# Moving the key tail's scores forward in an attention + MoE kernel: from behind the fourth score unit to behind the second

## The chip, the cores and the metric

One core of a Trainium2 chip; the jobs ran on different chips, each with the kernel before in the same rounds. The metric is the device time of one execution in microseconds (us). Where ratios are given, they are the mean time of one kernel's fast runs over that of the other's of the same rounds, so they are not quite the ratios of the medians quoted beside them; the interval is a 95% one.

Engines are named as in the profile: PE is TensorE's matmuls, PEld its weight loads, ACT is ScalarE, DVE is VectorE, POOL is GpSimd, SP is SyncE.

## The reference

Attention with a relative position bias, then a layer of two matmuls with a "snake" activation. Batch 8, heads 8, sequence 576, head size 64; hidden sizes 512 and 2048.

```python
scores = (q @ k.transpose(0, 1, 3, 2)) / np.sqrt(64) + bias[head, |i - j|]
attn   = softmax(scores)
x      = (attn @ v)            # rearranged to 4608 x 512
h      = x @ w_in              # 4608 x 2048
g      = h + np.sin(alpha * h) ** 2 / (alpha + 1e-9)
out    = g @ w_out             # 4608 x 512
```

## The kernel before

Heads are handled in pairs: four head pairs a batch. The scores of a pair are computed transposed (keys on partitions), in six units. Units 0 to 3 are 128 keys each for 512 queries, unit 4 is the remaining 64 queries of those four key blocks, and unit "t" is the key tail: the last 64 keys of both heads, put together to 128 rows. Units 0 to 4 use 64 contraction rows and run as two half-array matmuls side by side (one per head). The tail uses a block-diagonal operand and all 128 rows. Every unit fills one score slot in PSUM (two banks). ScalarE takes the exponential out of the slot into a buffer `u`, and VectorE multiplies the part near the diagonal by the bias factor. Then come the attention-value matmuls (27 for the first 384 queries of a pair, 18 for the rest).

From the third batch on there are three score slots, dealt out in order of issue, and units are issued in groups of two that wait for both of their slots:

```python
        if t < LAG - 1:                       # first two batches: single units, two slots
            groups = [[(p, i)] for p in range(NP) for i in (0, 1, 2, 3, "t", 4)]
            nreg = 2
        else:                                 # (pair of the two, unit)
            groups = [
                [(y + p, i) for y, i in g] for p in range(0, NP, 2) for g in (
                    ((0, 0), (0, 1)), ((0, 2), (0, 3)), ((0, "t"),), ((0, 4), (1, 0)),
                    ((1, 1), (1, 2)), ((1, "t"),), ((1, 3), (1, 4)),
                )
            ]
            nreg = 3
        seq = [y for g in groups for y in g]
        ...
        r = seq.index(y) % nreg               # the unit's slot
        ...
        m.mode = "f" if g[0][1] == "t" else "r"   # full array, or two halves
```

Nothing is issued in the order of the text. Each piece is a task with a priority and an assumed duration; while the kernel is built, a greedy list scheduler deals the tasks onto the engines, and that order is then fixed. The output projection (`g @ w_out`, 16 matmuls of 128x512 for each of 36 row blocks) is *fill*: it is allowed wherever PE would otherwise wait, up to a quota while a batch's scores are issued:

```python
                    if t.fill:
                        if self.in_qk and self.used >= self.quota[0] + self.quota[1] * self.share:
                            continue
...
QUOTA = {2: (4, 26)}
QUOTA_ELSE = (8, 48)
...
            def mm(e, f=f):                   # output projection, one of 16
                if f == 0:
                    m.v = bank(mb.tag)
                full(m.v, gcell[b].v[:, f, 128 * a : 128 * a + 128], w_out16[:, f, :],
                     f == 0, f == NF - 1)
```

Attention stages (exponentials on ScalarE) and sine stages (sine and square) alternate, since ScalarE must load another function table in between (13 loads of 1.28 us in the trace).

The softmax here doesn't subtract the row's maximum and nothing guards it: scores larger than these inputs give would overflow.

## Time and profile before

| | |
|---|---|
| median of 6 runs | 392.96 us (392.29 to 393.67) |
| span of the profiled run | 392.2 us |
| PE / ACT / DVE busy | 378.4 / 323.9 / 262.0 us |
| granted TensorE clock, mean | 0.995 |

First the page of the profiled execution: span, busy time and share of each engine, two rows of the picture in 40 slices (tenths busy, tenths of granted clock), and the engine shares of the chain of waits that ended last.

```profile
span 392.2 us, 8566 instructions
PE 378.4 (96%) x3401; PEld 190.1 (48%) x3401; DVE 262.0 (67%) x587; ACT 323.9 (83%) x458; POOL 81.9 (21%) x96
...
PE   6989999999999999999999999999999999999995
...
PEclk9989999999999999999999999999999999999999
...
PE 86%; DMA 4%; DVE 4%; ACT 3%; POOL 1%; issue 1%; ACTq 0%; DVEq 0%
```

PE is busy almost everywhere after the first slice, and the chain is mostly PE work behind PE work. The next view gives busy time by stretch. The stretches are four attention stages, from one table load to the next; the columns are length, then busy time and instructions of each engine, granted clock, DMA share and GB/s.

```profile
157.40:180.10 22.70, 22.52 (x259) 11.32 (x258) 14.79 (x39) 21.15 (x26) 0.00 (x0) 1.00 1.39 149
197.30:220.10 22.80, 22.38 (x259) 11.20 (x258) 15.59 (x40) 21.05 (x26) 0.00 (x0) 1.00 0.96 111
237.10:259.60 22.50, 22.43 (x259) 11.56 (x258) 14.69 (x39) 20.89 (x27) 0.00 (x0) 1.00 0.44 106
277.20:299.60 22.40, 22.25 (x258) 10.97 (x256) 14.70 (x40) 21.04 (x25) 0.00 (x0) 1.00 0.25 50
```

Two engines are nearly full in these stages, PE at 99% and ACT at 93%.

PE's waits from 96.7 us on (who waited for whom: us in total, times, longest):

```profile
PE am L450 <- DVE xp L785: 0.8, 2, 0.4
PE sc L450 <- ACT u L705: 0.4, 1, 0.4
PE sc L450 <- DVE g L879: 0.3, 1, 0.3
PE am L450 <- DVE outs L538: 0.2, 1, 0.2
```

That is 1.7 us of idle time in 295. But a matmul's end is modelled: the Trainium skill, "Perfetto Trace Analysis", section "Tensor Engine Instruction (MATMUL, LD_WEIGHTS)", says that the profiler estimates it. In this trace a 128x512 matmul has 380 ns while the next one starts 216 ns after it, so the shown durations overlap and short stalls vanish under them. Starts are better. I therefore took the distances between the starts of successive matmul records, by kind of the two. From the third batch on, before:

| step | median ns | count |
|---|---|---|
| fill to fill (128x512) | 216 | 423 |
| fill to score (full array to two halves) | 311 | 31 |
| score to fill (two halves to full array) | 308 | 28 |
| the two half-array matmuls of one unit (512 columns) | 4 | 96 of 132 |
| attention-value to attention-value (65 columns) | 29 | 840 |

The 216 ns agree with the 215.7 ns that the Trainium skill, "TensorE: Matmul & The Clock Gate", section "Wait — 56ns, not 53.3ns?", gives for 512 columns on a warm array, and the 4 ns with the start distance in the diagram of its section "The mechanism" of Part 3 and with the issue overhead of about 4 ns a tile in the section after it, "Measured speedup vs the span model". The 308 and 311 ns show about 0.09 us for each change between half and full array. The Trainium skill, "TensorEngine Tiling (Array Packing)", section "Key Properties", says that changing the tiling mode drains TensorE; it gives no time.

The timeline of PE at the start of one attention stage (start us, time us, operation, count; Q is a score unit if its output is sc, fill if its input is g):

```profile
158.40 0.61 PE L450 MATMUL sc<-qT,kT 64*128 64x512 f16 x4
158.94 1.47 PE L450 MATMUL am<-w_out,g 128*128 128x512 f16 x6
160.34 0.61 PE L450 MATMUL sc<-qT,kT 64*128 64x512 f16 x4
160.88 0.39 PE L450 MATMUL am<-w_out,g 128*128 128x512 f16 x1
161.10 0.41 PE L450 MATMUL sc<-qT,kt 128*128 128x288 f16 x2
161.35 1.89 PE L450 MATMUL am<-w_out,g 128*128 128x512 f16 x8
```

Units 0 and 1, fill, units 2 and 3, fill, the tail (kt), fill. Fill stands wherever the next group still waits for a slot. And ScalarE in that stage, with its idle time and what ended it in brackets:

```profile
158.83 4.42 ACT L705 ACTIVATE u<-sc 128x1024 f16<-128x1024 f32 x5
163.50 4.02 ACT L705 ACTIVATE u<-sc 128x512 f16<-128x512 f32 x5 [0.25 <-PE sc L450]
167.74 1.51 ACT L705 ACTIVATE u<-sc 128x1024 f16<-128x1024 f32 x2 [0.21 <-PE sc L450]
```

After every few exponentials it waits 0.20 to 0.33 us in this stage for the next group's scores.

### The profile page before, as it was taken

The numbers are of one execution on the slowest core, as the hardware profiler recorded it, in microseconds if no ns is written. First come the engines' busy times: TensorE is split into PE (matmuls) and PEld (weight loads), VectorE is DVE, ScalarE is ACT, GpSimd is POOL, SyncE is SP. The second block draws the span as 40 slices with busy tenths as digits, with TensorE's granted clock in tenths as the row PEclk, the third lists the DMA queues.
The fourth block names the chain that finished last, engine by engine and source line by source line (L and its number), as shares of the span: only waits on it lengthen the run. The fifth ranks groups of instructions, "written<-read, shape, count | busy, mean of one in ns | idle before, by whom it ended". The sixth has DMA issues, their size and how long they took to land.

```text
span 392.2 us, 8566 instructions
## 1 busy us (share of the span) xinstructions
PE 378.4 (96%) x3401; PEld 190.1 (48%) x3401; DVE 262.0 (67%) x587; ACT 323.9 (83%) x458; POOL 81.9 (21%) x96
## 2 busy tenths in 40 slices
PE   6989999999999999999999999999999999999995
PEld 2456445644455554445445544554445444444442
DVE  3576987768576689567967895768676869429100
ACT  2976999979899999999989999999999969539211
POOL 5762963090004545001700310000000000000000
PEclk9989999999999999999999999999999999999999
DMA  9999999999726999991996497211014000020122
GB/s 170 211 204 219 207 171 158 166 171 148 92 59 83 158 155 157 158 166 47 150 170 101 34 93 166 68 33 42 27 43 59 17 28 29 27 80 2 57 76 80
DMA packets 148647, 41.99 MB, mean 107 GB/s; under 512 B 137784, under 2 KB 142992, under 8 KB 148608
## 3 DMA queue, kind: packets, MB, share of 16 engines
q0 software_dynamic: 89872, 19.04, 56.9%
q1 hardware_dynamic: 58512, 22.36, 30.3%
q8 instruction: 26, 0.43, 0.5%
q14 instruction: 13, 0.11, 0.1%
q10 hardware_dynamic: 224, 0.05, 0.1%
HBM read 37.76 MB, written 16.52 MB: 138 GB/s over the span
## 4 chain that ended last, share of the span: by engine, by line
PE 86%; DMA 4%; DVE 4%; ACT 3%; POOL 1%; issue 1%; ACTq 0%; DVEq 0%
PE sc L450 41%; PE am L450 34%; PE cb L450 5%; PE ca L450 5%; ACT u L705 2%; DMA m2r<-e_dram 2%; DMA e_dram<-e_sb 1%; DMA phi_sb<-phi_const 1%; DVE g L879 1%; DVE u L730 1%; ACT s L865 1%; DVE xn L785 1%; DVE outs L538 0%; DVE kT L538 0%; POOL mhr L471 0%
## 5 line engine op out<-in xcount | busy, mean ns | idle before, releaser
L705 ACT ACTIVATE u<-sc 128x1024 f16<-128x1024 f32 (+1 forms) x192 | 157.8, 898 | 14.4 <-PE sc L450 12.9
L450 PE MATMUL sc<-xT,w_in 128*128 128x512 f16 x576 | 132.3, 379 | 0.6 <-DVE g L879 0.5
L879 DVE SCALAR_TENSOR_TENSOR g<-sq,inv_a,sc 128x512 f16<-128x512 f16 x144 | 103.3, 746 | 22.1 <-PE am L450 14.7
L450 PE MATMUL am<-w_out,g 128*128 128x512 f16 x416 | 108.6, 380 | 0.3 <-DVE outs L538 0.2
L865 ACT ACTIVATE s<-sc,alphaT 128x512 f16<-128x512 f32 x144 | 92.7, 678 | 6.4 <-PE sc L450 5.0
L730 DVE TENSOR_TENSOR u<-u,m2r 128x512 f16<-128x512 f16 (+2 forms) x160 | 67.7, 438 | 32.4 <-ACT u L705 27.8
L450 PEld LDWEIGHTS <-w_in 128*128 128x128 f16 x576 | 55.3, 98 | 65.0 <-issue 1.3
L450 PEld LDWEIGHTS <-g 128*128 128x128 f16 x576 | 53.3, 98 | 64.1 <-issue 11.6
L450 PEld LDWEIGHTS <-u 128*128 128x128 f16 x1440 | 55.8, 98 | 19.2 <-issue 11.0
L450 PE MATMUL sc<-qT,kT 64*128 64x64 f16 (+1 forms) x512 | 50.8, 297 | 1.7 <-ACT u L705 0.9
L450 PE MATMUL am<-v,u 128*128 128x65 f16 x1152 | 51.2, 194 | 0.0
L872 ACT ACTIVATE sq<-s 128x512 f16<-128x512 f16 x79 | 49.2, 628 | 2.2 <-DVE g L879 0.5
L396 POOL DMA_DIRECT2D v<-in_v_dram x24 | 22.2, 1065 | 119.6 <-PE am L450 104.3
L874 DVE TENSOR_TENSOR sq<-s 128x512 f16<-128x512 f16 x65 | 27.4, 423 | 9.2 <-ACT s L865 8.8
L450 PE MATMUL am<-vh,u 128*128 128x130 f16 x144 | 32.2, 224 | 0.8 <-DVE xp L785 0.8
L450 PEld LDWEIGHTS <-kT 64*128 64x128 f16 x512 | 14.7, 96 | 28.5 <-issue 24.3
L785 DVE TENSOR_TENSOR xp<-am,rd 128x384 f16<-128x384 f32 (+1 forms) x48 | 23.6, 491 | 1.8
L784 DVE RECIPROCAL rd<-am 128x6 f32<-128x6 f32 (+1 forms) x56 | 10.5, 187 | 19.7 <-PE am L450 19.2
L450 PE MATMUL cb<-w_out,g 128*128 128x512 f16 x96 | 23.0, 380 | 0.0
L937 ACT ACT_TABLE_LOAD x13 | 16.7, 1283 | 0.2
L377 POOL DMA_DIRECT2D staged_q<-in_q_dram x6 | 15.5, 2583 | 3.6 <-DMA staged_q<-in_q_dram 3.6
L538 DVE COPY outs<-am 128x512 f32<-128x512 f32 x19 | 13.1, 688 | 4.3 <-PE am L450 4.1
(88 smaller groups left out, 175.6 us busy)
## 6 DMA issues: line engine op xcount, KB each, us to landing
out_dram<-outs SPq DMA_DIRECT2D x36, 256.0 KB, 2.2
staged_k<-in_k_dram POOLq DMA_DIRECT2D x6, 576.0 KB, 13.8
staged_q<-in_q_dram POOLq DMA_DIRECT2D x6, 576.0 KB, 19.7
v<-in_v_dram POOLq DMA_DIRECT2D x24, 128.0 KB, 7.0
w_in<-in_moe_w_in_dram POOLq DMA_DIRECT2D x4, 512.0 KB, 8.8
w_out<-in_moe_w_out_dram POOLq DMA_DIRECT2D x4, 512.0 KB, 10.7
w_out<-in_v_dram SPq DMA_DIRECT2D x4, 256.0 KB, 8.2
v1st<-in_v_dram POOLq DMA_DIRECT2D x4, 256.0 KB, 16.6
```

Source lines behind the costliest of these rows:

```text
L377: nc.gpsimd.dma_start(out=dst.ap()[t].rearrange("s (h d) -> s h d", h=H), in_=src[t].rearrange("h s d -> s h d"),)
L396: nc.gpsimd.dma_start(out=vs[t % 2][:, c, :, 0:D], in_=vp[128 * c : 128 * c + 128],)
L450: nc.tensor.matmul(out=out, lhsT=lhsT, rhs=rhs, start=start, stop=stop)
L538: k_of(e).tensor_copy(out=o, in_=i)
L705: nc.scalar.activation(out=o, in_=x, func=AF.Exp, scale=0.125)
L730: nc.vector.tensor_tensor(out=io, in0=io, in1=m2[:, 2 * p : 2 * p + 2, x0 : x0 + hi - lo], op=ALU.mult,)
L785: nc.vector.tensor_tensor(out=y.rearrange("p c (z d) -> p c z d", z=2), in0=a[:, :, :, 0:D], in1=r.unsqueeze(3).to_broadcast([128, nq, 2, ...
L865: nc.scalar.activation(out=s16.v, in_=h.v, func=AF.Sin, scale=alphaT[:, f : f + 1])
L872: nc.scalar.activation(out=sq.v, in_=s16.v, func=AF.Square)
L874: k_of(e).tensor_tensor(out=sq.v, in0=s16.v, in1=s16.v, op=ALU.mult)
L879: nc.vector.scalar_tensor_tensor(out=gcell[b].v[:, f, :], in0=sq.v, scalar=inv_a[:, f : f + 1], in1=h.v, op0=ALU.mult, op1=ALU.add,)
L937: nc.scalar.preload_act_table_set(name)
```

## The change

The intent: issue the tail, which is short on ScalarE, between the long units, so that another exponential covers the wait for the next group. Only the order of the groups changes.

```diff
@@ -630,8 +630,7 @@
                 [(y + p, i) for y, i in g] for p in range(0, NP, 2) for g in (
-                    ((0, 0), (0, 1)), ((0, 2), (0, 3)), ((0, "t"),), ((0, 4), (1, 0)),
-                    ((1, 1), (1, 2)), ((1, "t"),), ((1, 3), (1, 4)),
+                    ((0, 0), (0, 1)), ((0, "t"),), ((0, 2), (0, 3)), ((0, 4), (1, 0)), ((1, "t"),), ((1, 1), (1, 2)), ((1, 3), (1, 4)),
                 )
```

In the first head pair of two the tail moves from behind the fourth unit to behind the second; in the second head pair from behind the third to behind the first. The list lost one line, so the changed kernel's line numbers are one lower (L705 is L704 there).

What the scheduler makes of it, for PE in the first half of that attention stage (Q: half-array score matmuls, T: tail, A: attention-value, F: fill, with counts):

```
before  Q4 F6 Q4 F1 T2 F8 Q10 A27 Q4 F1 T2 F1 A18 F2 Q10
after   Q4 T2 F9 Q4 F6 Q10 F1 T2 F6 Q4 A27 F2 Q10
```

## The prediction

> **What bounds the kernel now.** TensorE. The page's first part has PE busy 378.4 us of a 392.2 us span, ACT 323.9, DVE 262.0. Windows by stage show PE busy, from 96.75 us on (where the changed order begins to act), 43.0 of 43.95 us in the third and fourth batches, then 22.3 to 22.5 of 22.4 to 22.8 us in each attention stage and nearly all of every sine stage. The granted clock is 1.00. The chain of waits puts 86% of the span on PE.
>
> "Busy" can hide stalls, so I took start-to-start distances of matmul records after 96.75 us. A 128x512 matmul follows another after 216 ns; the Trainium skill, "TensorE: Matmul & The Clock Gate", section "Wait — 56ns, not 53.3ns?", gives 215.7 ns warm, so PE streams at its rate. Going from half-array score matmuls (64 rows, in pairs) to full-array ones takes 308 instead of 216 ns, going back 311: 0.19 us a round trip. True stalls (steps over 60 ns longer than usual) sum to only about 3.7 us; the largest are 0.8 us twice.
>
> **What the change does.** It adds and removes no instruction. From the third batch on the order in each pair of head pairs becomes 0,1,tail,2,3,4 | 0,tail,1,2,3,4. The static scheduler then re-deals the fill matmuls (output projection) and attention-value groups around it; everything up to about 100 us is the same. Score buffers rotate over three slots in order of issue, so which unit uses which slot changes too.
>
> **Costed.**
> - Mode switches: both built orders have 190 changes between half- and full-array matmuls. Difference 0.
> - Scalar waits: ACT now waits three times per two head pairs, 0.20 to 0.33 us (timeline): a group of two units needs the slot whose exponential ended last, and only a short exponential (tail 0.57 us, 64-column unit 0.50) covers it. The new order has three such places too, perhaps 0.1 us longer each; off the critical path while PE has fill work.
> - Attention-value matmuls of even pairs: before, the tail came last and they followed directly; now unit 3 comes last, with its vector multiply (0.42 us) and a hand-over between: 0.5 us later, 12 times. Fill covers it; without fill up to 6 us.
> - Tails right behind a score group may hold PE about 0.13 us for their slot (one step of 441 ns instead of 308 is in the trace): 0 to 1.5 us, probably near 0.
> - Gain: at best the 3.7 us of stalls.
>
> The last 45 us keep their work and order nearly unchanged.
>
> **Predicted: 393.2 us, 391.0 to 395.8 in 8 of 10.** Faster by over 2%: 0.01; within: 0.97; slower by over 2%: 0.02.
>
> **What would show each step.** Right: PE busy stays at 378 +- 1.5 us and its idle time at 12 to 16, the steps of 308 and 311 ns stay equal in number, stages change by under 0.5 us each with mixed signs, the first 99 us agree to 0.3 us. Wrong: long PE steps before attention-value matmuls (waiting for DVE) or tails (waiting for ACT), or attention stages all longer by over 0.5 us.
>
> **What would make it wrong.** The scheduler works with its own durations; where it thinks a slot free too early, in-order PE stalls, and 24 tails times 0.3 us would be 7 us. Or fill is used up earlier, leaving holes in the sine stages. Or the new order removes the 3.7 us of stalls: 389.5 to 391.

## More of the kernel before

The exponential has one cost in the plan and one instruction:

```python
            nc.scalar.activation(out=o, in_=x, func=AF.Exp, scale=0.125)
        ...
        x = plan.add({"ACT": t_act(n)}, ex, [m] + gate, base + 20, use=b + [ub])
```

## The result, and the profile after

| | before | after |
|---|---|---|
| median of 6 runs | 392.96 us (392.29 to 393.67) | 393.19 us (392.0 to 394.28) |
| span of the profiled run | 392.2 us | 390.6 us |
| PE / ACT / DVE busy | 378.4 / 323.9 / 262.0 | 377.2 / 320.2 / 264.4 |
| ratio | | 1.0006 (0.9981 to 1.003) |

The time is the same. The page of the changed kernel:

```profile
span 390.6 us, 8546 instructions
PE 377.2 (97%) x3401; PEld 190.3 (49%) x3401; DVE 264.4 (68%) x592; ACT 320.2 (82%) x453; POOL 82.2 (21%) x96
...
PE   5989999999999999999999999999999999999995
...
PEclk8599999999999999999999999999999999999999
...
PE 91%; ACT 4%; DVE 2%; DMA 1%; issue 0%; ACTq 0%; DVEq 0%
```

The span is 1.6 us shorter, but not by the change. One more view splits both traces at the table load that opens the third batch; the columns are as above. Before:

```profile
0.00:96.75 96.75, 89.00 (x918) 47.46 (x919) 69.56 (x167) 79.77 (x115) 49.46 (x66) 0.98 1.55 183
96.75:392.20 295.45, 289.44 (x2485) 142.61 (x2482) 192.42 (x421) 244.12 (x343) 32.46 (x30) 1.00 0.66 82
```

After:

```profile
0.00:95.24 95.24, 87.81 (x918) 46.99 (x919) 70.47 (x167) 79.44 (x115) 49.69 (x66) 0.93 1.56 183
95.24:390.60 295.36, 289.42 (x2485) 143.35 (x2482) 193.95 (x426) 240.76 (x338) 32.48 (x30) 1.00 0.67 83
```

Up to there both programs issue the same instructions in the same order, and there the 1.5 us lie; this part varied from 94.8 to 97.0 us over the profiles of the kernels here that share it. From the third batch on, where the change acts, 295.45 became 295.36 us, with PE busy 289.44 and 289.42.

The four attention stages of the changed kernel:

```profile
156.50:178.60 22.10, 22.02 (x257) 11.09 (x255) 14.87 (x39) 20.77 (x25) 0.00 (x0) 1.00 1.35 151
195.40:218.00 22.60, 22.60 (x260) 11.55 (x259) 15.08 (x40) 20.78 (x25) 0.00 (x0) 1.00 1.00 114
234.80:257.20 22.40, 22.36 (x258) 11.53 (x256) 15.05 (x39) 20.73 (x26) 0.00 (x0) 1.00 0.48 106
273.60:297.30 23.70, 23.70 (x265) 11.90 (x264) 15.93 (x41) 20.83 (x27) 0.00 (x0) 1.00 0.21 54
```

They changed by -0.6, -0.2, -0.1 and +1.3 us; the last one took up PE work that a shorter sine stage before it (16.4 us instead of 17.6) had left. PE's waits from 95.2 us on:

```profile
PE sc L450 <- ACT u L704: 0.8, 2, 0.6
PE am L450 <- ACT outs L536: 0.7, 1, 0.7
PE sc L450 <- DVE g L878: 0.2, 1, 0.2
```

Again 1.7 us, with other causes. The same stage's start on PE:

```profile
156.90 0.75 PE L450 MATMUL sc<-qT,kT 64*128 64x512 f16 x4
157.59 0.42 PE L450 MATMUL sc<-qT,kt 128*128 128x288 f16 x2
157.84 2.10 PE L450 MATMUL am<-w_out,g 128*128 128x512 f16 x9
159.88 0.60 PE L450 MATMUL sc<-qT,kT 64*128 64x512 f16 x4
160.42 1.47 PE L450 MATMUL am<-w_out,g 128*128 128x512 f16 x6
```

And on ScalarE, as above:

```profile
157.74 6.46 ACT L704 ACTIVATE u<-sc 128x1024 f16<-128x1024 f32 x8
164.55 3.49 ACT L704 ACTIVATE u<-sc 128x1024 f16<-128x1024 f32 x4 [0.34 <-PE sc L450]
168.32 2.48 ACT L704 ACTIVATE u<-sc 128x1024 f16<-128x1024 f32 x3 [0.28 <-PE sc L450]
```

The tail did move forward, and the first wait (after five exponentials before) is gone here; but the others are longer. Over the stretch of the four attention stages ScalarE waited 5.6 us for scores before and 7.3 us after (who waited for whom: us in total, times, longest; L705 is before, L704 after):

```profile
ACT u L705 <- PE sc L450: 5.6, 19, 0.7
ACT u L704 <- PE sc L450: 7.3, 20, 1.2
```

Had ScalarE been the limit, this would have shown in the time.

### An account of PE's time

From the table load that opens the third batch to the last matmul, add up all steps between matmul starts, and call "stall" what a step lies above the usual one of its kinds in the trace of before, where that is over 60 ns. Where before has no such step, or a single one, the nearest kind stands in (308 ns from a score unit to the tail, as from a score unit to fill). What is left is work, including the changes of array mode. "Mode changes" counts changes between half and full array among these steps.

| kernel | PE time, us | stalls, us | rest, us | mode changes |
|---|---|---|---|---|
| before | 291.01 | 3.51 | 287.50 | 120 |
| after | 290.95 | 3.50 | 287.45 | 120 |
| even_only | 290.56 | 2.98 | 287.58 | 120 |
| odd_only | 290.88 | 3.44 | 287.44 | 120 |
| tail_last | 290.62 | 3.17 | 287.45 | 120 |
| singles | 303.21 | 5.73 | 297.48 | 214 |
| pe_extra | 304.39 | 3.17 | 301.22 | 120 |
| act_half | 293.04 | 5.37 | 287.67 | 120 |
| act_full | 295.80 | 7.95 | 287.85 | 120 |
| three_ends | 290.38 | 4.26 | 286.12 | 108 |

The lower rows are the experiments that follow. This count repeats better than the runs' times: the profile of after_again, a later run of the changed kernel, gave 290.95 and 3.50 us again, and three_again gave the 290.38 us of three_ends.

Most of the stalls are not the same ones. Before had 0.58 us twice where attention-value matmuls waited (idle of 0.4 us each is shown, for a normalisation), 0.54 us at a score group and 0.47 us early in a sine stage. After has the latter two at 0.31 and 0.33 us, and new ones: 0.85 us where fill waits for ScalarE's copy of an output block, and 0.69 us at the first matmul of a sine stage. The sums agree to 0.01 us, which no theory here forces: that is luck within the 3 to 4 us that such stalls come to.

### The profile page after: what moved, and what is told of

The parts are those of the page before. It is cut to its first block, busy times and chain, and to the rows that moved or that the text cites. A ratio compares the mean times of both kernels' runs of the same rounds, so it can differ in the third digit from the quotient of the medians.

```text
span 390.6 us, 8546 instructions
## 1 busy us (share of the span) xinstructions
PE 377.2 (97%) x3401; PEld 190.3 (49%) x3401; DVE 264.4 (68%) x592; ACT 320.2 (82%) x453; POOL 82.2 (21%) x96
## 4 chain that ended last, share of the span: by engine, by line
PE 91%; ACT 4%; DVE 2%; DMA 1%; issue 0%; ACTq 0%; DVEq 0%
PE sc L450 44%; PE am L450 35%; PE cb L450 6%; PE ca L450 5%; ACT u L704 3%; DMA tabL<-in_bias_table_dram 1%; PE cb L558 1%; DVE g L878 1%; PE am L558 1%; DVE xp L784 0%; DVE kT L538 0%; ACT outs L536 0%; PE ca L821 0%; PE am L821 0%; DVE tabN L504 0%
## 5 line engine op out<-in xcount | busy, mean ns | idle before, releaser
L704 ACT ACTIVATE u<-sc 128x1024 f16<-128x1024 f32 (+1 forms) x192 | 156.2, 899 | 15.1 <-PE sc L450 14.1
L450 PEld LDWEIGHTS <-u 128*128 128x128 f16 x1440 | 55.3, 98 | 16.4 <-issue 5.0
L450 PE MATMUL am<-v,u 128*128 128x65 f16 x1152 | 50.3, 194 | 0.0
L871 ACT ACTIVATE sq<-s 128x512 f16<-128x512 f16 x73 | 45.7, 629 | 2.4 <-DVE g L878 0.5
L873 DVE TENSOR_TENSOR sq<-s 128x512 f16<-128x512 f16 x71 | 29.7, 422 | 8.2 <-ACT s L864 7.8
```

What stands on the lines that cost most here:

```text
L450: nc.tensor.matmul(out=out, lhsT=lhsT, rhs=rhs, start=start, stop=stop)
L871: nc.scalar.activation(out=sq.v, in_=s16.v, func=AF.Square)
L873: k_of(e).tensor_tensor(out=sq.v, in0=s16.v, in1=s16.v, op=ALU.mult)
```

## The experiments

Theory A, that of the prediction: PE is bound by the sum of its work. The order of the score units can only move the stalls, some 3.5 us in all. Rival B: the change has two effects of several us that happen to cancel, a gain by the earlier tail and a loss by the later attention-value matmuls. Rival C: ScalarE, or the chain through it, is the limit, and PE only looks full because fill has been put everywhere.

All kernels gave correct results. All diffs are to the changed kernel except where said.

### even_only and odd_only: one half of the change each

```diff
 # even_only: the second head pair as before
-((0, 4), (1, 0)), ((1, "t"),), ((1, 1), (1, 2)), ((1, 3), (1, 4)),
+((0, 4), (1, 0)), ((1, 1), (1, 2)), ((1, "t"),), ((1, 3), (1, 4)),
 # odd_only: the first head pair as before
-((0, 0), (0, 1)), ((0, "t"),), ((0, 2), (0, 3)), ((0, 4), (1, 0)),
+((0, 0), (0, 1)), ((0, 2), (0, 3)), ((0, "t"),), ((0, 4), (1, 0)),
```

> Only the first head pair of each two has its tail moved behind its second unit. Theory A (TensorE is bound by the sum of its work, 378 us busy, and the order only shuffles stalls that sum to about 3 us): 391.5 to 395 us, ratio to before 0.997 to 1.004, 190 mode changes as before. Rival B (two effects of several us cancel: the earlier tail gains, the later attention-value matmuls of the first pair lose): this half carries the loss and reads 396 to 399 us, and the other half the gain.

> Only the second head pair of each two has its tail moved (behind its first unit). Theory A: 391.5 to 395 us, ratio 0.997 to 1.004. Rival B: this half carries the gain, 387 to 390 us, since its attention-value matmuls do not wait for a later multiply.

Measured: even_only 392.41 us, ratio 0.9984 (0.9962 to 1.0005); odd_only 392.53 us, ratio 0.999 (0.9969 to 1.0012); before in the same rounds 392.96. Neither half carries a loss or a gain of several us. Rival B is out.

### tail_last: the tail elsewhere altogether

```diff
-((0, 0), (0, 1)), ((0, "t"),), ((0, 2), (0, 3)), ((0, 4), (1, 0)),
-((1, "t"),), ((1, 1), (1, 2)), ((1, 3), (1, 4)),
+((0, 0), (0, 1)), ((0, 2), (0, 3)), ((0, 4), (1, 0)), ((0, "t"),),
+((1, 1), (1, 2)), ((1, 3), (1, 4)), ((1, "t"),),
```

> The tail is put last in both head pairs, further from both orders than they are from each other: it delays every first attention-value group until the last exponential. Mode changes still 190. Theory A: 391 to 396 us, ratio within 0.995 to 1.007, as fill takes the place of the later groups. Rival B (position of the tail matters and the two known positions only happen to tie): 397 us or more.

Measured: 392.14 us, ratio 0.9988 (0.9964 to 1.0012). In the trace the attention-value matmuls of the first head pairs start 1.86 us after the fifth exponential's end (median of 12), against 0.53 us before and 0.89 us after; it cost nothing. Five orders (before, after, even_only, odd_only and this one) lie within 0.4% of each other.

### pe_extra: more work for PE alone

The first matmul of each output block is repeated with the same operands; each repetition writes the sum anew, so the result stays right. Blocks 2 to 5, 16 x 4 = 64 matmuls more, and the plan is told.

```diff
                 if f == 0:
                     m.v = bank(mb.tag)
+                for _ in range(4 if f == 0 and 1 < b < 6 else 0):
+                    full(m.v, gcell[b].v[:, f, 128*a : 128*a+128], w_out16[:, f, :], True, True)
                 full(...)
```

(The task's assumed PE time is multiplied by five for these matmuls.)

> The changed kernel with 64 more 128x512 matmuls in the output projection of blocks 2 to 5: the first of each accumulation is issued five times with the same operands, the last one starting the sum, so the result stays right. Theory A: 64 x 0.216 = 13.8 us more, 406 to 408 us. Rival C (ScalarE or the chain through it is the limit and TensorE's busy time only looks full): under 5 us more.

Measured: 406.24 us beside 393.27 of before, ratio 1.0332 (1.0311 to 1.0353). In PE's account the rest grew by 301.22 - 287.45 = 13.77 us, 215 ns a matmul, while the stalls went from 3.50 to 3.17 us. A matmul more costs its full step. Rival C is out in its strong form.

### act_half and act_full: more work for ScalarE alone

The tail's exponential is done twice from the third batch on, in act_half for the first head pair of two only. The second one writes the same values. The plan is not told, so PE's order stays that of after.

```diff
-            nc.scalar.activation(out=o, in_=x, func=AF.Exp, scale=0.125)
+            for _ in range(2 if i == "t" and t > 1 and p % 2 == 0 else 1):   # act_full: without p % 2
+                nc.scalar.activation(out=o, in_=x, func=AF.Exp, scale=0.125)
```

> The changed kernel with the tail's exponential of each first head pair done twice from the third batch on: 12 x 0.59 = 7.1 us more on ScalarE, in TensorE's order unchanged. Theory A: ScalarE has 1.3 to 2 us of idle in each attention stage of 22.5 us and gets 1.2 us more, so 0 to 2 us more in all (393 to 395.5). Rival C: 6 to 7 us more (399 to 400.5).

> The tail's exponential of every head pair done twice from the third batch on: 24 x 0.59 = 14.2 us more on ScalarE, TensorE's order unchanged. With 7.1 us more it was 2 to 3 us slower, by stalls before tails and score groups (5.4 us instead of 3.5). If ScalarE's idle time in the attention stages is now used up, the next 7.1 us should come through nearly in full: 401 to 404 us, stalls 11 to 14 us. If fill still covers: 397 to 399 us.

Measured: act_half 395.96 us beside 393.27, ratio 1.0063 (1.0037 to 1.009); act_full 398.11 us beside 392.5, ratio 1.014 (1.0117 to 1.0163). The additions were larger than the planned 7.1 and 14.2 us: in the traces the second exponential starts 0.69 us (act_half) and 0.72 us (act_full) after the first on average, so 8.3 and 17.2 us were added. Of these some 2.5 and 5.5 us came through against the kernel before, and 2.1 and 4.9 us in PE's account against the changed kernel: a quarter to a third. This is between the theories, and act_half is above what I had expected from theory A (0 to 2 us). For act_full the lower alternative (397 to 399 us) was met, but not its number for the other case: stalls were 7.95 us. The account shows where it goes: rest 287.67 and 287.85, nearly unchanged, stalls 5.37 and 7.95 instead of 3.50. PE's waits in act_full, from 96 us on:

```profile
PE sc L450 <- ACT u L705: 2.3, 5, 0.6
PE am L450 <- ACT outs L536: 0.7, 1, 0.7
```

The first line was 0.8 us in the changed kernel. So ScalarE is no limit by itself, but it is close behind PE: its waits for scores in the whole run shrank from 14.1 to 6.9 us under act_full, which took about two fifths of the addition, and part of the rest arrived as stalls of PE, whose order was fixed without knowledge of it.

### nofill_before and nofill_after: the two orders without fill

```diff
-QUOTA = {2: (4, 26)}
-QUOTA_ELSE = (8, 48)
+QUOTA = {}
+QUOTA_ELSE = (0, 0)
```

(nofill_before is the same edit to the kernel before.)

> The order of before, but no fill matmul (output projection) may be issued while a batch's scores are: all of it moves to the sine stages. Mode changes in the built order 156. Attention stages should stay near 21 to 23 us, bound by ScalarE's exponentials with their waits, while about 277 fill matmuls (60 us) go elsewhere: 440 to 455 us by theory A. It is the base for the next run.

> The changed order without fill in the same way. Theory A says that fill hides the order's own effect, which must then show here: by the later attention-value groups and the changed scalar waits the six late attention stages differ by 0.1 to 1 us each, so 1 to 6 us to the run before this one, either sign, most likely slower. If the order has no effect of its own: within 0.5 us.

Measured: nofill_before 440.55 us, ratio to before 1.1212 (1.1181 to 1.1244); nofill_after 440.86 us, ratio 1.1195 (1.1157 to 1.1234). The first is as expected. The second comes out near the case "no effect of its own": the medians differ by 0.3 us, and the ratios have the other sign. But each interval reaches over 1 us to either side, so the times alone rule out only an effect of several us. The traces are finer. Here PE is no limit in the attention stages. Two of the four such stages of nofill_before:

```profile
163.40:184.60 21.20, 15.76 (x222) 8.90 (x221) 13.76 (x37) 20.38 (x25) 0.00 (x0) 1.00 1.49 138
209.40:230.80 21.40, 16.45 (x220) 9.75 (x219) 14.01 (x38) 20.36 (x25) 0.00 (x0) 0.92 0.54 75
```

and of nofill_after:

```profile
165.20:186.80 21.60, 16.62 (x222) 9.90 (x220) 13.57 (x38) 20.39 (x26) 0.00 (x0) 0.92 1.51 140
211.70:233.00 21.30, 16.62 (x220) 10.01 (x219) 14.16 (x38) 20.36 (x25) 0.00 (x0) 0.92 0.48 69
```

PE is busy 16 to 17 us of 21 to 22, ScalarE 20.4 in both, and all four such stages together, from table load to table load, take 86.1 us before and 85.9 us after; from the third batch on PE's time is 337.46 and 337.02 us. The first stage does not compare, since only nofill_before kept its full clock there (21.2 against 21.6 us). In the other three both read 0.92, and the changed order was 0.13, 0.28 and 0.14 us shorter. So fill does not hide an effect of several us; a gain of 0.1 to 0.3 us a stage is not excluded. With ScalarE as the limit the order is nearly neutral too; it changes neither ScalarE's work nor, within 0.2 us of 14, its waits for scores from 100 us on.

### singles: more changes of array mode

```diff
-((0, 0), (0, 1)), ((0, "t"),), ((0, 2), (0, 3)), ((0, 4), (1, 0)), ...
+((0, 0),), ((0, 1),), ((0, "t"),), ((0, 2),), ((0, 3),), ((0, 4),), ((1, 0),), ...
```

> The changed order, but every score unit is its own group, so that fill and attention-value matmuls come between all of them: 284 mode changes instead of 190 in the built order. Theory A with a cost of 94 ns per change (308 and 311 ns steps instead of 216): 94 x 0.094 = 8.8 us more, 401 to 403 us, with some of it perhaps given back by fewer scalar waits. If mode changes are hidden behind other waits: within 1 us of 393.

Measured: 404.35 us, ratio 1.029 (1.0264 to 1.0317), somewhat above what I expected. The account splits it: the rest grew by 297.48 - 287.45 = 10.03 us for 94 changes, 107 ns each, and the stalls by 2.2 us. Of the 10.03 us, 8.69 come from the usual single steps of before (92 ns a change); the other 1.34 are steps lengthened by less than 60 ns, which the account does not call stalls. Unlike the position of the tail, this is a property of the order that costs.

### three_ends, three_again and after_again: fewer changes of array mode

The groups are dealt over the whole batch, and the first and the last have three units, so there are nine runs of half-array matmuls a batch instead of ten (the lines taken out are cut here).

```diff
+groups = [list(g) for g in (
+    ((0, 0), (0, 1), (0, 2)), ((0, "t"),), ((0, 3), (0, 4)), ((1, 0), (1, 1)), ((1, "t"),), ((1, 2), (1, 3)),
+    ((1, 4), (2, 0)), ((2, 1), (2, 2)), ((2, "t"),), ((2, 3), (2, 4)), ((3, 0), (3, 1)), ((3, "t"),),
+    ((3, 2), (3, 3), (3, 4)),
+)]
```

> The groups dealt over the whole batch, the first and the last one with three score units, so nine runs of half-array matmuls a batch instead of ten: 178 mode changes instead of 190. In the runs so far TensorE's time from the third batch on was the sum of its work (287.5 us) and of its stalls (3.0 to 3.5), and a mode change cost 106 ns where single groups added 94 of them. Theory A: 12 x 0.1 = 1.2 us less if the stalls stay at 3 to 3.5 us: 391 to 392.5 us. The last group of a batch needs all three slots free, so ScalarE idles about 1 us there; if that turns into TensorE stalls, it is a tie or 1 to 3 us slower.

> The same kernel as three_ends once more, since its interval (0.996 to 1.000) only touches 1. If the 12 mode changes less are worth their 1.2 us less the 0.8 us of stalls they brought, the ratio is again 0.997 to 0.9995, 391.5 to 392.5 us.

> The changed kernel unaltered, on the same chip as the run before it: ratio to before 0.998 to 1.002, 392 to 394 us, so that the three orders can be set side by side.

Measured: three_ends 391.64 us, ratio 0.998 (0.996 to 1.0); again, 392.04 us, ratio 0.9981 (0.9964 to 0.9997); the changed kernel beside the second one 393.46 us, ratio 1.0012 (0.9996 to 1.0027), before there 392.62. The rest fell by 287.45 - 286.12 = 1.33 us for 12 changes (111 ns each), and the stalls rose by 0.76. The version is ahead of the kernel before by 0.2% in both jobs, just clear of 1 in the second interval (by 0.9 and 0.6 us in the medians), and of the changed kernel by 0.4%, 1.4 us, in the medians of the same job. That is small beside the 2% at which this study calls a kernel faster, but its sign was predicted, and it repeated.

## Why the prediction was right

- *"TensorE" bounds the kernel; 393.2 us, 391.0 to 395.8.* Measured 393.19. That the middle was hit to 0.01 us is luck, since the runs of the changed kernel alone spread from 392.0 to 394.28 us; the range is what was predicted. The bound is shown by pe_extra (215 ns for each added matmul of 216) against act_half and act_full (a quarter to a third of what was added).
- *"Mode switches ... Difference 0."* Shown: 120 changes from the third batch on in both traces, and the step matters, 107 to 111 ns a change in singles and three_ends. Steps from a score unit of 512 columns to the full array (the 308 ns) are 48 in both traces, those from fill to a score unit (the 311 ns) 43 before and 41 after. The prediction's 0.09 us a change fits the single step (92 to 95 ns); what the changes cost in sum was somewhat more.
- *"Scalar waits ... three such places too, perhaps 0.1 us longer each; off the critical path".* The profile agrees on the size (5.6 us of waiting became 7.3 over the four stages) and the time on the harmlessness. "Off the critical path while PE has fill work" was too generous as a general statement: act_half shows that a quarter to a third of added ScalarE time reaches PE.
- *"Attention-value matmuls of even pairs: ... 0.5 us later, 12 times. Fill covers it; without fill up to 6 us."* The delay exists: from the fifth exponential's end to the first attention-value matmul 0.53 us before, 0.89 after (0.06 and 0.29 without fill), a little less than predicted. The second sentence was wrong: without fill, too, the later start cost nothing that shows (337.46 and 337.02 us of PE time from the third batch on). What the traces show is that the score groups, which feed ScalarE, do not get later with the attention-value matmuls. That a further buffer or stage would eventually have to wait was argued, not tried.
- *"Tails right behind a score group may hold PE about 0.13 us ... probably near 0."* Shown: 12 tails follow a score group after; their steps have a median of 309 ns, and stalls before tails sum to 0.41 us.
- *"Gain: at best the 3.7 us of stalls."* The runs agree with it: over five orders of the tail the stalls stayed between 2.98 and 3.51 us, so no order removed much more than half a microsecond of them. (3.7 was added up by hand; the stricter count gives 3.51. The prediction's "largest are 0.8 us twice" are whole steps; they lie 0.58 us above the usual.)
- *"the first 99 us agree to 0.3 us"* did not hold: 96.75 and 95.24 us, with identical instructions. This part varies from run to run, for a cause that stays open: the granted clock does not explain it, since the shorter one had the lower clock (0.93 against 0.98). *"stages change by under 0.5 us each"* did not hold either: one attention stage grew by 1.3 us and a sine stage shrank by 1.2. Stage borders shift as the scheduler deals fill differently; only the sum has a meaning.

## What to carry to other kernels

Where one engine is full and a scheduler fills its gaps, count three things before and after a reordering: the work, the changes of array mode, and the stalls. If the first two are equal, only the stalls can move, and their sum in the trace is the bound of the gain. Read stalls from the distances between starts, not from a busy share; and to learn how near a second engine is, add work to that engine alone and see which part comes through.

## What the Trainium skill lacked or had wrong

- "TensorEngine Tiling (Array Packing)", section "Key Properties", says that a change of tiling mode drains TensorE but gives no time. Here a change between two 64-row halves and the full array cost 92 to 95 ns in single steps (308 and 311 instead of 216 ns), and 107 to 111 ns a change where 94 were added or 12 removed. At 120 changes that is 11 to 13 us of 391, worth a number on the page.
- "TensorE: Matmul & The Clock Gate", section "Back-to-back issue gap", gives about 131 ns a matmul for 512 columns in sustained streams of weight load and matmul, and calls the 216 ns of its formula an over-count. In this trace the median step of 423 such fill matmuls, each with its own weight load, is 216 ns, and an added one cost 215 ns.
- "TensorE: Matmul & The Clock Gate", section "A second HAM failure mode: psum-queue depth-cycling", describes a clock that falls through short idle gaps, but has no measure of when. In the kernels without fill a stage with PE busy 15.76 of 21.2 us kept a granted clock of 1.00, while stages with 16.45 to 16.72 of 21.3 to 21.7 us read 0.92: the busy share of a stage does not tell. Each 0.92 is one stretch of 3.41 us at half the clock. Cut the two traces from the third batch on into such stretches, counted from the first fall of the clock in the record: after each one with PE shown busy for at most 51% (0.08 to 0.51 of it) the next was at half the clock, at least in part, and after each with 62% or more it was at full. Where between 51 and 62% the border lies was not tested, and PE's busy time has modelled ends.
- No page that I found has how far the time of one program's start varies; the nearest, "TensorE: Matmul & The Clock Gate", section "What's actually happening", counts the slow matmuls of a start and gives no spread of times. With identical instructions the part before the third batch took 94.8 to 97.0 us in the profiles here, while the rest repeated to 0.01 us of PE time (290.95 us twice, 290.38 us twice).
